# More score blocks turned by DMA, and z turned by overlapping twos, in a gated attention and token mixing kernel

## The chip, the core and the metric

The kernel runs on one core of one Trainium2 chip. The metric is the device time of one execution in microseconds; the median of several runs is compared. The core has the engines PE (TensorE: matmuls), DVE (VectorE), ACT (ScalarE), POOL (GpSimd) and SP (SyncE, which here only issues DMAs), and 16 DMA engines that all queues share. PEld in a profile is TensorE's loading of weights, which overlaps its matmuls.

## The reference

Eight batches (B), 3200 rows each (S), D = 256 columns; z and the two key projections have 64 columns.

```python
scores = (1 / S) * z @ z.T                  # S x S, symmetric
attn   = np.maximum(scores, 0.0) ** 2       # symmetric too
x      = u * (attn @ v)                     # S x D
wq, wk = x @ w_q, x @ w_k                   # S x 64
mixed  = ((1 / 8) * wq @ wk.T) @ x          # computed as wq @ (wk.T @ x)
out    = np.maximum(mixed, 0.0) @ w_out
```

All inputs and the output are float32; the kernel works in float16 with float32 sums. Since `attn` is symmetric, the block of rows i and columns j is the transpose of the block of rows j and columns i.

## The kernel before

**Tiling.** The 3200 rows of a batch are 25 tiles of 128 (row tiles). The columns of `attn` are cut into seven groups: six of 512 and a last one of 128 (`widths`, `starts`; `LASTG` is 6). For each batch `b` and group `gi`, all 25 row tiles are summed into the group's output: 4 x 25 = 100 steps of the second product for a full group, 25 for the last. One step is a pair of matmuls on the two halves of TensorE's rows, 64 rows each (`second_product`, line 332).

**Scores.** A score tile is 128 rows by the 512 columns of a group. Two tiles form a pair `p`; `scores` (line 247) gives one to the upper 64 rows of TensorE and one to the lower 64. For that z must stand transposed in both halves: `zT[b]`. The pair is evacuated by `first_stage` (ReLU, line 269 on ACT or 273 on DVE) and squared into float16 by `second_stage` (line 289 on ACT or 291 on POOL) into a buffer `at` of the pool `pat` (`NAT` = 14 pairs).

**Turned blocks.** Where `is_turned(b, gi, gj)` holds, the score tiles of group gi whose rows belong to group gj are also transposed by DMA on SP's queue (line 311), and serve as the tiles of group gj whose rows belong to gi, which are then not computed. Before the change it holds for groups one and two apart (`FAR` = 2) and for every group with the last. The turned blocks stand in buffers `tt1` (3), `tt2` (4) and `ttl` (8); a full block is 4 KiB in each partition.

**z of the next batches.** `load_z` brings z of batch b+1 by a converting DMA from POOL's queue, `double_z` copies it twice on DVE into `zd` (line 161), so that each tile stands there twice side by side, and `turn_z` transposes it in five DMAs of five tiles (line 167), which gives each tile in both halves at once.

**The rest of a group.** `gate` adds the two halves' sums (ACT line 348, DVE line 349) and multiplies by u (POOL line 370) into x. `turn_x` transposes x by DMA (line 384), `projections` (line 401) makes queries and keys, `turn_keys` (line 419) transposes the keys by DMA, POOL doubles them (line 431), `heads` (line 438) sums keys times x. When a batch is through, `mix` (line 466) and `proj` (line 493) make the output, ACT scales it (line 521), SP stores it (line 522). u is loaded by SP (line 175), v by POOL's queue (line 150).

**Order of the work.** The program is straight-line: a planner in Python runs through it while it is built, with a clock for each engine, SP's queue (`sp_at`) and the DMA engines (`dma_at`), and writes out each engine's instructions in the order that its estimates give. `use_pair` issues a pair of scores, `acc_step` a step of the second product. A transfer on SP is given to `move(ready, due, issue, takes, fn, landed, may)`; `flush` sends those that are ready, the earliest due first, and those with `may` only when that holds. `out_of[p]` counts transposes of pair p that have not landed; pair p may be produced only when the buffer of pair p - `NAT` is used up and turned. Scores run ahead of the second product: the pair is wanted when `p * total < (done_acc + lead) * NPAIR`, with `lead` = 140 steps.

Of the kernel before, what the change touches and what calls it, by code (L numbers as in the profile page):

```python
# [16 lines left out]
def kernel(  # L17
# [15 lines left out]
    P = 128  # L33
# [17 lines left out]

    NAT = 14
    NX = 6
    NEARBY = 8
# [7 lines left out]
    pk = ctx.enter_context(tc.tile_pool(name="pk", bufs=3))  # L62
    pxt = ctx.enter_context(tc.tile_pool(name="pxt", bufs=3))
    pu = ctx.enter_context(tc.tile_pool(name="pu", bufs=2))
# [21 lines left out]

    zT, vs, us, xs, xTs, qks, ks, hacc, hss, rts, zds = ({} for _ in range(11))

# [7 lines left out]
    z32 = {}  # L96
    zd0 = pz.tile([P, NT, 2, dqk], FP16, tag="zd", name="zd")
    vs[0] = pv.tile([P, NT, D], FP16, tag="v_sb", name="v_sb")
    zT[0] = pzt.tile([P, S], FP16, tag="zT2", name="zT2")

# [50 lines left out]

    zdense, ztimes = {}, []

    def load_z(b):
        zdense[b] = pz.tile([P, NT, dqk], FP16, tag="zn", name="zn")
        nc.gpsimd.dma_start(out=zdense[b][:], in_=rows(z, b))

    def double_z(b, half):
        if half == 0:
            zds[b] = pz.tile([P, NT, 2, dqk], FP16, tag="zd", name="zd")  # L160
        nc.vector.tensor_copy(out=zds[b][:, :, half, :], in_=zdense[b][:])

    def turn_z(b, i):
        ztimes.append((b, i))
        if i == 0:
            zT[b] = pzt.tile([P, S], FP16, tag="zT2", name="zT2")
# [11 lines left out]

    wq32 = consts.tile([P, NC, dh], FP32, tag="wq32", name="wq32")
    wk32 = consts.tile([P, NC, dh], FP32, tag="wk32", name="wk32")  # L180
    wqk = consts.tile([P, NC, 2, dh], FP16, tag="wqk", name="wqk")
# [57 lines left out]
    NPAIR = NTILE // 2  # L239
    made, turned = {}, {}  # L240

    def scores(p):
        assert len(ztimes) >= 5 * tiles[2 * p + 1][0] and p_chunk(p) in z_at, (p, clock, len(ztimes), z_at)
        sc = ps_tile("sc")
        for h, (b, gi, ti) in enumerate(tiles[2 * p : 2 * p + 2]):
            gs, gw = starts[gi], widths[gi]
            nc.tensor.matmul(  # L247
                out=sc[:, h, 0:gw],
                lhsT=zT[b][top(h), ts(ti, P)],
                rhs=zT[b][top(h), ds(gs, gw)],  # L250
                start=True,
                stop=True,
            )
        return sc
# [24 lines left out]
    def second_stage(p, g, ways):  # L279
        at = pat.tile([P, 2 * W], FP16, tag="at", name="at")  # L280
        at0 = 0
        parts = pieces(p)
        if len(ways) > len(parts):
            parts = [(slice(h, h + 1), parts[0][1]) for h in range(2)]
        for (hs, w), on_act in zip(parts, ways * 2):
            n = hs.stop - hs.start
            out = at[:, at0 : at0 + n * w].rearrange("p (n w) -> p n w", w=w)
            if on_act:
                nc.scalar.square(out=out, in_=g[:, hs, 0:w])  # L289
            else:  # L290
                nc.gpsimd.tensor_mul(out=out, in0=g[:, hs, 0:w], in1=g[:, hs, 0:w])  # L291
# [12 lines left out]
        def turn(b, gi, gj, n0, nn, c0, c1):  # L304
            if (b, gi, gj) not in turned:
                kind, nr, bufs = ("l", 1, 8) if gj == LASTG else (gj - gi, 4, gj - gi + 2)
                turned[b, gi, gj] = ptt.tile(
                    [P, nr, 4, P], FP16, tag=f"tt{kind}", name=f"tt{kind}", bufs=bufs
                )
            out = turned[b, gi, gj][:].rearrange("p n j t -> p (n j) t")  # L310
            nc.sync.dma_start_transpose(out=out[:, 4 * n0 : 4 * (n0 + nn), :], in_=at[:, c0:c1])

        return [(x, lambda x=x: turn(*x)) for x in blocks]
# [28 lines left out]
    def gate(b, gi, half):  # L342
# [9 lines left out]
        if b == last and gi >= LASTG - 2:  # L352
            if gi == LASTG - 2 and half == 0:
                spare = pz.tile([P, NT, 2, dqk], FP16, tag="zd", name="xd")
                spare = spare[:].rearrange("p n a k -> p (n a k)")
                spare = spare[:, 0 : 9 * D].rearrange("p (n d) -> p n d", d=D)
                for i in range(3):
                    xds[LASTG - 2 + i] = spare[:, 4 * i : min(4 * i + 4, 9), :]
# [21 lines left out]
    def turn_x(b, gi):  # L380
        assert len(xTs) < 3
        n = min(2, widths[gi] // P)
# [190 lines left out]
    sp_at, dma_at = [0.0], [0.0]  # L573
    LANDS = 4.0
    RING = 2.0
    SLACK = 1.0
# [41 lines left out]
    def cold():  # L618
        return 2.0 if clock[PE] < 8.4 else 1.0

    SPLIT = 0.2
    UNTIL = 24.0
# [27 lines left out]
    def squares():  # L650
        while pending and pending[0][0] <= clock[PE] + 0.3:
# [9 lines left out]
            for (b, gi, gj, _, nn, _, _), turn in second_stage(p, g, ways):  # L661
                n = nn * widths[gi] // P
                due = done + (4.0 if gj == gi + 1 else 9.0)
                out_of[p] = out_of.get(p, 0) + 1
                move(done + SLACK, due + SLACK, 1.28, 0.21 * n, turn, lambda t, x=(p, b, gi, gj, nn): block_landed(t, *x))
            for x in tiles[2 * p : 2 * p + 2]:
# [16 lines left out]
    def use_keys(b, gi):  # L683
# [15 lines left out]
        if not final:  # L699
            move(  # L700
                done + SLACK, done + 10.0, 1.28, 0.21 * n, lambda: turn_keys(b, gi),
                lambda t: at_time(t, lambda: double(b, gi)),
# [48 lines left out]
    def use_proj(b, gi):  # L751
# [12 lines left out]

        move(done + SLACK, done + 6.0, 0.55, 1.6, stores[0], landed)

# [3 lines left out]

    Z0 = 24
    V0 = 56
    V1 = 11

    def batch_begun(b, t):
        if b + 1 < B:
            t0 = max(t + 6, Z0)
            at_time(t0, lambda: (load_z(b + 1), push(3.0)))
            for half in range(2):
                at_time(  # L780
                    t0 + 12 + 3 * half,
                    lambda half=half: (double_z(b + 1, half), give(DVE, clock[PE], 0.98)),
                )
            step = 6 if b else 4
            for i in range(5):
                move(
                    t0 + 18 + step * i, t0 + 34 + step * i, 1.28, 1.05,
                    lambda i=i: turn_z(b + 1, i),
# [6 lines left out]
    def v_loaded(b, n0, nn):  # L795
        load_v(b, n0, nn)
        push(2.5)
        for n in range(n0, n0 + nn):
# [4 lines left out]
    def z_here(p):  # L803
        b = tiles[2 * p + 1][0]
        return not b or z_ready.get((b, 4), 1e9) <= clock[PE]

    def group_begun(b, gi, t):
        if gi == 0:
            batch_begun(b, t)
        if gi + 1 < NG:  # L810
            move(max(t + 2, clock[POOL] + SLACK), t + 7, 0.55, 1.6, lambda: load_u(b, gi + 1))
        elif b + 1 < B:
            move(max(t + 2, clock[POOL] + SLACK), t + 7, 0.55, 1.6, lambda: load_u(b + 1, 0))

    SPARE = 0.3
    BIAS = 0.2
    XDUE = 5.0
    XWAIT = 3.0
    LATE = 0.3
# [3 lines left out]
    def half_done(b, gi, half):  # L823
# [10 lines left out]
        elif half == halves(gi)[-1]:  # L834
            n = 8 if widths[gi] == W else 2
            move(
                t + SLACK, t + XDUE, 1.28, 0.21 * n, lambda: turn_x(b, gi),
                lambda t: x_landed(t, b, gi), lambda: len(xTs) < 3,
            )
# [54 lines left out]
    def acc_step():  # L894
# [59 lines left out]
    at_time(10.0, lambda: turn_first(3))  # L954
    move(10.0, 14.0, 0.55, 1.6, lambda: load_u(0, 0))
    load_weights()
# [3 lines left out]
    done_acc = 0  # L960
    lead = 140
    turn_about = False
    while groups or work or current["left"]:
# [134 lines left out]
```

## Time and profile before

| | before |
|---|---|
| median of 3 runs | 784.35 us (782.85 to 785.14) |
| profiled execution | 784.44 us |
| its span, first to last instruction | 782.7 us |
| granted TensorE clock | 0.999 |
| PE / PEld busy | 769.8 / 663.7 us |
| DVE / ACT / POOL busy | 503.3 / 546.4 / 645.1 us |
| transposes on SP: tt, ttl, xT_sb, kx, zT | 143, 48, 56, 53, 35 |
| DMA | 140.88 MB, 180 GB/s in the mean |

The profile is one execution. Busy time is the union of an engine's instructions. A group's row gives the line, the engine, the operation, output and inputs, the count, then busy us, the mean ns of one, and the engine's idle time just before these instructions with what ended it. The chain of work that ended last follows the span back from its end through what released each step. Transposes are issued on SP ("SPq"): the duration shown there is that of issuing; "to landing" is from issue until the data is there.

### The profile page before, as it was taken

The page shows a single profiled execution, that of the slowest core. Times are in us where ns is not written, and L with a number is a line of the kernel's source. Part 1 is how long each engine was busy: PE and PEld are TensorE (multiplying, and loading weights), DVE is VectorE, ACT ScalarE, POOL GpSimd, SP SyncE. Part 2 cuts the span into 40 slices and gives each one's busy share as a digit, 9 for nine tenths or more (in the row PEclk, how much of TensorE's full clock was granted, in tenths as well). Part 3 has the DMA queues.
Part 4 walks back from the last instruction along what each step waited for, and adds up shares of the span by engine and source line. Part 5 has one row for each costly group of instructions (what it writes and reads, how often), then busy time and mean ns, then how long its engine had stood idle before and what let it go on. Part 6 is the DMA issues. An engine that isn't in the chain of part 4 may idle for free.

```text
span 782.7 us, 28343 instructions
## 1 busy us (share of the span) xinstructions
PE 769.8 (98%) x12410; PEld 663.7 (85%) x12410; DVE 503.3 (64%) x515; ACT 546.4 (70%) x663; POOL 645.1 (82%) x530
## 2 busy tenths in 40 slices
PE   7999999999999999999999999999999999999996
PEld 5899999788899878888889887998889888898784
DVE  6766556655587556786476665777567556566635
ACT  6868777668676767766677767776678676777534
POOL 7898988788889877888789889778788879888961
PEclk9999999999999999999999999999999999999999
DMA  7999999999999999999799989999999998969635
GB/s 179 143 174 170 157 181 180 165 175 206 216 174 177 211 184 189 185 212 189 180 177 174 220 173 201 168 164 217 190 188 152 183 228 166 202 127 210 142 59 213
DMA packets 306300, 140.88 MB, mean 180 GB/s; under 512 B 285056, under 2 KB 287744, under 8 KB 306176
## 3 DMA queue, kind: packets, MB, share of 16 engines
q1 hardware_dynamic: 299408, 122.90, 82.1%
q0 software_dynamic: 6624, 15.98, 15.0%
q8 instruction: 97, 1.59, 0.9%
q10 hardware_dynamic: 144, 0.20, 0.1%
q14 instruction: 27, 0.22, 0.1%
HBM read 59.64 MB, written 26.21 MB: 110 GB/s over the span
## 4 chain that ended last, share of the span: by engine, by line
PE 92%; DVE 2%; DMA 1%; ACT 1%; POOL 1%; issue 1%; DVEq 0%; SPq 0%; ACTq 0%
PE acc L332 67%; PE sc L247 13%; PE fo L493 6%; PE qk L401 3%; PE qk L438 2%; PE mx L466 1%; DVE g L273 1%; DMA v_sb<-in_v_dram 1%; POOL at L291 1%; ACT g L269 1%; ACT at L289 0%; DMA z<-in_z_dram 0%; DVE fo L516 0%; PE hd L438 0%; DVE both L349 0%
## 5 line engine op out<-in xcount | busy, mean ns | idle before, releaser
L291 POOL TENSOR_TENSOR at<-g 128x1024 f16<-128x1024 f32 (+2 forms) x252 | 457.1, 1827 | 62.4 <-DVE g L273 50.3
L332 PE MATMUL acc<-v_sb,at 64*128 64x256 f16 x7344 | 498.4, 269 | 1.2 <-DMA v_sb<-in_v_dram 0.7
L273 DVE TENSOR_SCALAR g<-sc 128x1024 f32<-128x1024 f32 (+2 forms) x320 | 372.6, 1178 | 135.3 <-PE sc L247 126.7
L332 PEld LDWEIGHTS <-at 64*128 64x128 f16 x7344 | 400.9, 94 | 55.2 <-issue 8.1
L289 ACT ACTIVATE at<-g 128x1024 f16<-128x1024 f32 (+2 forms) x230 | 228.1, 1008 | 19.2 <-DVE g L273 17.0
L269 ACT ACTIVATE g<-sc 128x1024 f32<-128x1024 f32 (+2 forms) x159 | 156.5, 986 | 67.1 <-PE sc L247 58.5
L247 PE MATMUL sc<-zT 64*128 64x512 f16 x924 | 187.6, 377 | 1.9 <-DVE g L273 0.8
L370 POOL TENSOR_TENSOR x_sb<-both,u_sb 128x512 f16<-128x512 f32 (+1 forms) x112 | 134.7, 1209 | 43.9 <-DVE both L349 43.6
L332 PE MATMUL acc<-v_sb,tt 64*128 64x256 f16 x2272 | 159.2, 269 | 0.0
L332 PEld LDWEIGHTS <-tt 64*128 64x128 f16 x2272 | 123.5, 94 | 14.3
L349 DVE TENSOR_TENSOR both<-acc,both 128x512 f32<-128x512 f32 (+1 forms) x104 | 69.7, 670 | 86.4 <-ACT both L348 73.3
L348 ACT COPY both<-acc 128x512 f32<-128x512 f32 (+1 forms) x104 | 59.0, 568 | 70.7 <-PE acc L332 66.4
L247 PEld LDWEIGHTS <-zT 64*128 64x128 f16 x924 | 60.8, 94 | 12.9 <-issue 8.9
L521 ACT ACTIVATE fo<-fo 128x1024 f32<-128x1024 f32 (+1 forms) x48 | 44.6, 930 | 24.3 <-PE fo L493 23.8
L493 PE MATMUL fo<-wo,rt 128*128 128x256 f16 x400 | 53.2, 274 | 1.3 <-ACT rt L481 0.5
L483 ACT ACTIVATE rt<-mx 128x1024 f16<-128x1024 f32 (+1 forms) x49 | 45.6, 934 | 11.5 <-PE mx L466 11.2
L414 ACT CAST qk<-qk 128x512 f16<-128x512 f32 (+1 forms) x54 | 29.4, 544 | 30.0 <-PE qk L438 24.1
L493 PEld LDWEIGHTS <-rt 128*128 128x128 f16 x400 | 34.9, 98 | 15.8 <-issue 10.9
L453 DVE TENSOR_TENSOR ha<-qk,ha 128x512 f32<-128x512 f32 x37 | 25.6, 691 | 30.7 <-ACT qk L414 30.2
L401 PE MATMUL qk<-xT_sb,wqk 64*128 64x256 f16 (+1 forms) x404 | 32.4, 265 | 0.0
L431 POOL COPY kx<-kx 128x128 f16<-128x128 f16 (+1 forms) x99 | 26.2, 294 | 5.7 <-DMA kx<-qk 5.7
L438 PE MATMUL qk<-x_sb,kx 64*128 64x256 f16 x342 | 28.4, 269 | 0.0
(45 smaller groups left out, 233.7 us busy)
## 6 DMA issues: line engine op xcount, KB each, us to landing
u_sb<-in_u_dram SPq DMA_DIRECT2D x48, 512.0 KB, 4.9
out_dram<-fo SPq DMA_DIRECT2D x47, 512.0 KB, 5.2
v_sb<-in_v_dram POOLq DMA_DIRECT2D x35, 320.0 KB, 5.5
zn<-in_z_dram POOLq DMA_DIRECT2D x7, 400.0 KB, 6.8
tt<-at SPq DMA_TRANSPOSE x143, 4.3
u_sb<-in_u_dram SPq DMA_DIRECT2D x8, 128.0 KB, 3.1
out_dram<-fo SPq DMA_DIRECT2D x8, 128.0 KB, 3.4
xT_sb<-x_sb SPq DMA_TRANSPOSE x56, 5.8
```

Of the source, the lines that this page charges most:

```text
L247: nc.tensor.matmul(out=sc[:, h, 0:gw], lhsT=zT[b][top(h), ts(ti, P)], rhs=zT[b][top(h), ds(gs, gw)], start=True, stop=True,)
L269: nc.scalar.activation(out=g[:, hs, 0:w], in_=sc[:, hs, 0:w], func=RELU, scale=GSCALE)
L273: nc.vector.tensor_scalar(out=g[:, hs, 0:w], in0=sc[:, hs, 0:w], scalar1=0.0, scalar2=GSCALE, op0=AOP.max, op1=AOP.mult,)
L289: nc.scalar.square(out=out, in_=g[:, hs, 0:w])
L291: nc.gpsimd.tensor_mul(out=out, in0=g[:, hs, 0:w], in1=g[:, hs, 0:w])
L332: nc.tensor.matmul(out=accs[half, r][:, ds((j % 2) * D, D)], lhsT=weights(b, gi, ti, j)[top(r), :], rhs=vs[b][top(r), ti, :], start=(first ...
L348: nc.scalar.copy(out=both[:, 0 : n * D], in_=accs[half, 0][:, 0 : n * D])
L349: nc.vector.tensor_add(out=both[:, 0 : n * D], in0=accs[half, 1][:, 0 : n * D], in1=both[:, 0 : n * D])
L370: nc.gpsimd.tensor_mul(out=xs[b, gi][:, 0:n, :, r, :].rearrange("p n c d -> p (n c) d"), in0=both[:, 0 : n * D].rearrange("p (m d) -> p m ...
L401: nc.tensor.matmul(out=ps[:, r, 0 : n * P], lhsT=wqk[top(r), c, :, :].rearrange("p t h -> p (t h)"), rhs=xTs[b, gi][top(r), 0:n, c, :], st ...
L483: nc.scalar.activation(out=out, in_=ps[:, 0:nr, 0 : ND * n * P], func=RELU)
L493: nc.tensor.matmul(out=banks[r][:, ds(j * D, D)], lhsT=flat[:, ds((dc * n + j) * P, P)], rhs=wo[:, dc, :], start=(dc == 0 and j == 0), sto ...
```

## The change

- `EXTRA`: in batches 1 to 7 the blocks (0,3), (1,4), (2,5) and (0,4) are turned too; the score tiles that they stand for are not computed.
- **Homes.** Full turned blocks of every distance share `NHOME` = 7 buffers. A turn is sent only when its block has a home or one is free (`has_home`); the home comes back when the planner has issued the last step that reads the block (`give_home_back`).
- **z.** The copies on DVE are gone. z is loaded into one buffer `zn` with an empty tile before and after it (set to zero once, on POOL). Four transposes take twos of neighbouring tiles: those beginning at an even place, and those at an odd one. So each tile stands once in the upper and once in the lower half, the upper one 128 columns further on (`z_cols`).
- **Buffers.** `NAT` 14 to 16, `NX` 6 to 7, turned x 3 to 4 (`NXT`). The first batch's doubled z and the last x share the pool of v, the query and key weights that of the output tiles.
- **Planner.** The cost of a transposed block is 0.17 instead of 0.21 (`BLOCK`), of u and output rows 1.3 instead of 1.6 (`ROWS4`), of the v and z loads 1.8 and 2.2 instead of 2.5 and 3.0. Blocks three or four groups apart are due 12 us after their square. x waits 7 instead of 3 us before its keys. A pair is wanted by its place in its own group (`need`) instead of evenly over the run.

```diff
-    NAT = 14
-    NX = 6
+    NAT = 16
+    NX = 7
+    NXT = 4
...
     def load_z(b):
-        zdense[b] = pz.tile([P, NT, dqk], FP16, tag="zn", name="zn")
-        nc.gpsimd.dma_start(out=zdense[b][:], in_=rows(z, b))
-
-    def double_z(b, half):
-        if half == 0:
-            zds[b] = pz.tile([P, NT, 2, dqk], FP16, tag="zd", name="zd")
-        nc.vector.tensor_copy(out=zds[b][:, :, half, :], in_=zdense[b][:])
+        nc.gpsimd.dma_start(out=zn[:, 1 : NT + 1, :], in_=rows(z, b))
...
+    ZTURNS = [(0, 0, 7), (1, 0, 7), (0, 7, 13), (1, 7, 13)]
     def turn_z(b, i):
+        odd, m0, m1 = ZTURNS[i]
...
         nc.sync.dma_start_transpose(
-            out=zT[b][:].rearrange("p (n s) -> p n s", s=P)[:, 5 * i : 5 * i + 5, :],
-            in_=zds[b][:, 5 * i : 5 * i + 5, :, :].rearrange("p n a k -> p (n a k)"),
+            out=zT[b][:].rearrange("p (m o s) -> p o m s", o=2, s=P)[:, odd, m0:m1, :],
+            in_=zn[:, 2 * m0 + odd : 2 * m1 + odd, :].rearrange("p n k -> p (n k)"),
         )
+
+    def z_cols(b, h, at, n):
+        return zT[b][top(h), ds(at + (P if b and h == 0 else 0), n)]
...
     SKIP = [(0, 2)]
+    EXTRA = [(0, 3), (1, 4), (2, 5), (0, 4)]
     def is_turned(b, gi, gj):
         if b == 0 and (gi, gj) in SKIP:
             return False
+        if b and (gi, gj) in EXTRA:
+            return True
         return gi < gj and (gj <= gi + FAR or gj == LASTG)
...
+    NHOME = 7
+    homes, homes_free = {}, list(range(NHOME))
+
+    def has_home(b, gi, gj):
+        return gj == LASTG or (b, gi, gj) in turned or bool(homes_free)
+
+    def give_home_back(b, gj, t):
+        gi = group_of(t)
+        if (b, gi, gj) in homes and all(
+            (b, gj, starts[gi] // P + n) in used for n in range(widths[gi] // P)
+        ):
+            homes_free.append(homes.pop((b, gi, gj)))
...
-                lhsT=zT[b][top(h), ts(ti, P)],
-                rhs=zT[b][top(h), ds(gs, gw)],
+                lhsT=z_cols(b, h, ti * P, P),
+                rhs=z_cols(b, h, gs, gw),
...
-                kind, nr, bufs = ("l", 1, 8) if gj == LASTG else (gj - gi, 4, gj - gi + 2)
+                if gj == LASTG:
+                    tag, nr, bufs = "ttl", 1, 8
+                else:
+                    homes[b, gi, gj] = home = homes_free.pop(0)
+                    tag, nr, bufs = f"tt{home}", 4, 1
...
-                due = done + (4.0 if gj == gi + 1 else 9.0)
+                due = done + {1: 4.0, 2: 9.0}.get(gj - gi, FARDUE)
...
+                    lambda x=(b, gi, gj): has_home(*x),
...
-    XWAIT = 3.0
+    XWAIT = 7.0
...
         used.add(row)
+        if row:
+            give_home_back(*row)
...
+    for p in range(NPAIR):
+        b, gi, _ = tiles[2 * p]
+        i0, i1 = first_of[b, gi], ends[b, gi]
+        n = NT * (widths[gi] // P)
+        need.append(steps[b, gi] + STRETCH * n * (2 * p - i0) / (i1 - i0))
...
-        wanted = able and p * total < (done_acc + lead) * NPAIR
+        wanted = able and need[p] < done_acc + lead
```

`steps[b, gi]` is the number of second-product steps ahead of that group, `first_of` and `ends` are the places of a group's first and last tile in the list.

More of the change, by code (lines that the diff above doesn't have):

```diff
@@ L85 @@
     ctx.enter_context(tc.manual_schedule())
-    zT, vs, us, xs, xTs, qks, ks, hacc, hss, rts, zds = ({} for _ in range(11))
+    zT, vs, us, xs, xTs, qks, ks, hacc, hss, rts = ({} for _ in range(10))
     def rows(t, b):
@@ L96 @@
     z32 = {}
-    zd0 = pz.tile([P, NT, 2, dqk], FP16, tag="zd", name="zd")
+    zd0 = pv.tile([P, NT, 2, dqk], FP16, tag="v_sb", name="zd")
     vs[0] = pv.tile([P, NT, D], FP16, tag="v_sb", name="v_sb")
-    zT[0] = pzt.tile([P, S], FP16, tag="zT2", name="zT2")
+    zT[0] = pzt.tile([P, S + P], FP16, tag="zT2", name="zT2")
+    zn = pz.tile([P, NT + 2, dqk], FP16, tag="zn", name="zn")
     def load_first_z():
@@ L150, in load_v @@
         nc.gpsimd.dma_start(out=vs[b][:, n0 : n0 + nn, :], in_=rows(v, b)[:, n0 : n0 + nn, :])
[L152 removed]
+    ztimes = []
+    ZTURNS = [(0, 0, 7), (1, 0, 7), (0, 7, 13), (1, 7, 13)]
     def load_z(b):
[L155 to L161 removed]
+        nc.gpsimd.dma_start(out=zn[:, 1 : NT + 1, :], in_=rows(z, b))
     def turn_z(b, i):
+        odd, m0, m1 = ZTURNS[i]
         ztimes.append((b, i))
         if i == 0:
[L166 removed]
+            zT[b] = pzt.tile([P, S + P], FP16, tag="zT2", name="zT2")
         nc.sync.dma_start_transpose(
[L168 to L170 removed]
+            out=zT[b][:].rearrange("p (m o s) -> p o m s", o=2, s=P)[:, odd, m0:m1, :],
+            in_=zn[:, 2 * m0 + odd : 2 * m1 + odd, :].rearrange("p n k -> p (n k)"),
+        )
+    def z_cols(b, h, at, n):
+        return zT[b][top(h), ds(at + (P if b and h == 0 else 0), n)]
     def load_u(b, gi):
@@ L175, in load_u @@
         nc.sync.dma_start(out=us[b, gi][:, 0:nn, :], in_=rows(u, b)[:, n0 : n0 + nn, :])
-    wq32 = consts.tile([P, NC, dh], FP32, tag="wq32", name="wq32")
-    wk32 = consts.tile([P, NC, dh], FP32, tag="wk32", name="wk32")
+    w32s = pg.tile([P, 2, W], FP32, tag="fo", name="w32s", bufs=2)
+    w32s = w32s[:, 0, :].rearrange("p (i c h) -> p i c h", i=2, h=dh)
+    wq32, wk32 = w32s[:, 0, :, :], w32s[:, 1, :, :]
     wqk = consts.tile([P, NC, 2, dh], FP16, tag="wqk", name="wqk")
@@ L240 @@
     made, turned = {}, {}
+    NHOME = 7
[8 more added lines that the diff above has]
+            homes_free.append(homes.pop((b, gi, gj)))
     def scores(p):
-        assert len(ztimes) >= 5 * tiles[2 * p + 1][0] and p_chunk(p) in z_at, (p, clock, len(ztimes), z_at)
+        assert len(ztimes) >= 4 * tiles[2 * p + 1][0] and p_chunk(p) in z_at, (p, clock, len(ztimes), z_at)
         sc = ps_tile("sc")
@@ L305, in turn @@
             if (b, gi, gj) not in turned:
-                kind, nr, bufs = ("l", 1, 8) if gj == LASTG else (gj - gi, 4, gj - gi + 2)
-                turned[b, gi, gj] = ptt.tile(
-                    [P, nr, 4, P], FP16, tag=f"tt{kind}", name=f"tt{kind}", bufs=bufs
-                )
+                if gj == LASTG:
[3 more added lines that the diff above has]
+                    tag, nr, bufs = f"tt{home}", 4, 1
+                turned[b, gi, gj] = ptt.tile([P, nr, 4, P], FP16, tag=tag, name=tag, bufs=bufs)
             out = turned[b, gi, gj][:].rearrange("p n j t -> p (n j) t")
@@ L353, in gate @@
             if gi == LASTG - 2 and half == 0:
-                spare = pz.tile([P, NT, 2, dqk], FP16, tag="zd", name="xd")
-                spare = spare[:].rearrange("p n a k -> p (n a k)")
-                spare = spare[:, 0 : 9 * D].rearrange("p (n d) -> p n d", d=D)
+                spare = pv.tile([P, NT, D], FP16, tag="v_sb", name="xd")
                 for i in range(3):
@@ L380, in turn_x @@
     def turn_x(b, gi):
-        assert len(xTs) < 3
+        assert len(xTs) < NXT
         n = min(2, widths[gi] // P)
@@ L574 @@
     LANDS = 4.0
+    BLOCK = 0.17
+    ROWS4 = 1.3
     RING = 2.0
@@ L619, in cold @@
         return 2.0 if clock[PE] < 8.4 else 1.0
+    FARDUE = 12.0
     SPLIT = 0.2
@@ L662, in squares @@
                 n = nn * widths[gi] // P
-                due = done + (4.0 if gj == gi + 1 else 9.0)
+                due = done + {1: 4.0, 2: 9.0}.get(gj - gi, FARDUE)
                 out_of[p] = out_of.get(p, 0) + 1
-                move(done + SLACK, due + SLACK, 1.28, 0.21 * n, turn, lambda t, x=(p, b, gi, gj, nn): block_landed(t, *x))
+                move(
+                    done + SLACK, due + SLACK, 1.28, BLOCK * n, turn,
+                    lambda t, x=(p, b, gi, gj, nn): block_landed(t, *x),
+                    lambda x=(b, gi, gj): has_home(*x),
+                )
             for x in tiles[2 * p : 2 * p + 2]:
@@ L763, in landed @@
             stored[i] = t
-        move(done + SLACK, done + 6.0, 0.55, 1.6, stores[0], landed)
+        move(done + SLACK, done + 6.0, 0.55, ROWS4, stores[0], landed)
     def push(takes):
@@ L771 @@
     Z0 = 24
+    ZWAIT, ZDUE, ZSTEP, ZSTEP0 = 14.0, 32.0, 7.0, 5.0
     V0 = 56
@@ L777, in batch_begun @@
             t0 = max(t + 6, Z0)
[L778 to L785, printed above, removed]
+            if b == 0:
+                nc.gpsimd.memset(zn[:, 0 : NT + 2 : NT + 1, :], 0.0)
+            at_time(t0, lambda: (load_z(b + 1), push(2.2)))
+            step = ZSTEP if b else ZSTEP0
+            for i, (_, m0, m1) in enumerate(ZTURNS):
                 move(
-                    t0 + 18 + step * i, t0 + 34 + step * i, 1.28, 1.05,
+                    t0 + ZWAIT + step * i, t0 + ZDUE + step * i, 1.28, BLOCK * (m1 - m0),
                     lambda i=i: turn_z(b + 1, i),
@@ L796, in v_loaded @@
         load_v(b, n0, nn)
-        push(2.5)
+        push(1.8)
         for n in range(n0, n0 + nn):
@@ L804, in z_here @@
         b = tiles[2 * p + 1][0]
-        return not b or z_ready.get((b, 4), 1e9) <= clock[PE]
+        return not b or z_ready.get((b, 3), 1e9) <= clock[PE]
     def group_begun(b, gi, t):
@@ L810, in group_begun @@
         if gi + 1 < NG:
-            move(max(t + 2, clock[POOL] + SLACK), t + 7, 0.55, 1.6, lambda: load_u(b, gi + 1))
+            move(max(t + 2, clock[POOL] + SLACK), t + 7, 0.55, ROWS4, lambda: load_u(b, gi + 1))
         elif b + 1 < B:
-            move(max(t + 2, clock[POOL] + SLACK), t + 7, 0.55, 1.6, lambda: load_u(b + 1, 0))
+            move(max(t + 2, clock[POOL] + SLACK), t + 7, 0.55, ROWS4, lambda: load_u(b + 1, 0))
     SPARE = 0.3
@@ L836, in half_done @@
             move(
-                t + SLACK, t + XDUE, 1.28, 0.21 * n, lambda: turn_x(b, gi),
-                lambda t: x_landed(t, b, gi), lambda: len(xTs) < 3,
+                t + SLACK, t + XDUE, 1.28, BLOCK * n, lambda: turn_x(b, gi),
+                lambda t: x_landed(t, b, gi), lambda: len(xTs) < NXT,
             )
@@ L954 @@
     at_time(10.0, lambda: turn_first(3))
-    move(10.0, 14.0, 0.55, 1.6, lambda: load_u(0, 0))
+    move(10.0, 14.0, 0.55, ROWS4, lambda: load_u(0, 0))
     load_weights()
@@ L961 @@
     lead = 140
+    STRETCH = 1.0
+    need, at, seen = [], 0, 0
+    steps = {}
+    for b in range(B):
+        for gi in range(NG):
+            steps[b, gi] = at
+            at += NT * (widths[gi] // P)
+    first_of = {}
+    for i, (b, gi, t) in enumerate(tiles):
+        first_of.setdefault((b, gi), i)
+    for p in range(NPAIR):
[3 more added lines that the diff above has]
+        need.append(steps[b, gi] + STRETCH * n * (2 * p - i0) / (i1 - i0))
     turn_about = False
```

4 lines of the change are left out of this document (2 added, 2 removed).

## The prediction

> **What bounds the kernel now.** I read the busy times first, then the chain of work that ended last, then the groups by line, the waits, the windows by stage, and last the queue of SP, because the change adds work there.
>
> ```profile
> PE 769.8 (98%) x12410; PEld 663.7 (85%) x12410; DVE 503.3 (64%) x515; ACT 546.4 (70%) x663; POOL 645.1 (82%) x530
> PE acc L332 67%; PE sc L247 13%; PE fo L493 6%; PE qk L401 3%; PE qk L438 2%; PE mx L466 1%; DVE g L273 1%; DMA v_sb<-in_v_dram 1%; POOL at L291 1%; ACT g L269 1%; ACT at L289 0%; DMA z<-in_z_dram 0%; DVE fo L516 0%; PE hd L438 0%; DVE both L349 0%
> ```
>
> 92% of that chain lies on TensorE: 67% in the second product (line 332), 13% in the scores (line 247). The other engines have room on average. The groups say whether TensorE waits for anybody:
>
> ```profile
> L332 PE MATMUL acc<-v_sb,at 64*128 64x256 f16 x7344 | 498.4, 269 | 1.2 <-DMA v_sb<-in_v_dram 0.7
> L332 PE MATMUL acc<-v_sb,tt 64*128 64x256 f16 x2272 | 159.2, 269 | 0.0
> L247 PE MATMUL sc<-zT 64*128 64x512 f16 x924 | 187.6, 377 | 1.9 <-DVE g L273 0.8
> L291 POOL TENSOR_TENSOR at<-g 128x1024 f16<-128x1024 f32 (+2 forms) x252 | 457.1, 1827 | 62.4 <-DVE g L273 50.3
> ```
>
> The idle column of the first three rows is 1.2, 0.0 and 1.9 us in the whole run: neither an evacuation nor a turned block (the `tt` row) makes TensorE wait. Most of the idle time lies at the two ends; one batch in the middle shows it, by the windows (columns: PE, weight loads, DVE, ACT, POOL, clock, DMA share, GB/s):
>
> ```profile
> 274.00:371.00 97.00, 97.00 (x1568) 82.15 (x1565) 67.12 (x67) 67.63 (x82) 81.19 (x66) 1.00 1.05 192
> 745.00:783.00 38.00, 31.09 (x430) 24.37 (x425) 17.71 (x23) 13.28 (x25) 12.46 (x14) 0.98 0.45 140
> ```
>
> TensorE is busy for all 97 us of the batch, at the full clock. A busy TensorE need not be at its peak, since matmuls overlap. The timeline of TensorE alone decides that (columns: start, us, instruction):
>
> ```profile
> 271.35 0.39 PE L247 MATMUL sc<-zT 64*128 64x512 f16 x2
> 271.57 1.36 PE L332 MATMUL acc<-v_sb,at 64*128 64x256 f16 x22
> 272.77 0.22 PE L466 MATMUL mx<-qk,hs 64*128 64x128 f16 x1
> ```
>
> A pair of score matmuls, whose halves run side by side, occupies 271.57 - 271.35 = 0.22 us. The 22 second-product matmuls after it take 1.20 us until the next starts, 0.109 us a pair. So 5000 pairs of the second product take 545 us and 462 pairs of scores 102 us. The order of instructions on each engine is written out by the planner before the run, so a score pair taken out closes the ranks behind it unless an operand comes late.
>
> **What it removes.** Group gi needs a score tile for each of 25 row tiles, less those it takes from an earlier group turned. By `is_turned` the counts by group are 25, 21, 17, 17, 17, 17, 1 (115 a batch), and with the four new blocks (0,3), (1,4), (2,5), (0,4) they are 25, 21, 17, 13, 9, 13, 1 (99). Sixteen tiles less in 7 batches are 112 tiles, 56 pairs; 924 matmuls become 812. The longer answer of the chain gives line 247 12.7% of 782.7 us, 99.4 us, which over 462 pairs is 0.215 us each; the timeline says 0.22. **56 x 0.215 = 12.0 us** (12.3 by the timeline). The second product is unchanged in number.
>
> The same 56 pairs leave the other engines: one first stage each (1221 ns on DVE or 1025 ns on ACT for 128x1024) and one square (1895 ns on POOL or 1055 ns on ACT). Also gone are 14 copies that double z on DVE, 975 ns each, 13.7 us. I count all of that at nothing: it lies beside TensorE, which waited 0.8 us on DVE there. It gives cover.
>
> A rule speaks against the price. The Trainium skill, Perfetto Trace Analysis, "Identifying the Most-Contended Engine", says that matmul busy time is no good measure of TensorE's headroom and that the busy share of weight loads is. By the page of the profile that share is 85%, and line 247's loads are busy for 60.8 us over 462 pairs, 0.13 us a pair, so by it the sum would be 56 x 0.13 = 7.4 us. The trace doesn't agree with it here, and I keep 0.215: the timeline shows that the missing loads are score pairs streaming 512 columns behind short loads, not idle time.
>
> **What it adds, all of it on SP and the DMA rings.** Each of the 28 new blocks is turned by two transposes of 128x1024:
>
> ```profile
> L311 SPq DMA_TRANSPOSE tt<-at x143: 1231/1267/5132, 18.6 to 724.4; - x143
> DMA to landing us min/median/max: 2.7/4.3/10.6
> SPq L311 <- POOL at L291: 42.4, 37, 5.1
> ```
>
> Columns of the first: issue time in ns, least, median and most. 56 more issues at 1.27 us are 71 us of SP; the z transposes go from 5 to 4 a batch (median 1287 ns), 7 x 1.29 = 9 us back. By the trace SP's issues fill 628 of 783 us now (mean 1.72 us for line 311: long ones are held up by full rings). At that mean the new total is 628 + 96 - 11 = 713 of 771 us, 92% instead of 80%. The packets' time, 98% of sixteen engines, isn't a capacity: stages run at 1.15 already (80 to 177 us). The blocks turned rise from some 2120 to 2570, a fifth.
>
> What hides it: a new block is made in group gi and read three or four groups later; a group lasts 97 / 6.25 = 15.5 us, so 30 us or more lie between, against 10.6 us for the slowest landing. Queued behind a waiting transpose on SP are the u loads, the x and key transposes and the stores. Their readers are POOL (line 370), TensorE (line 401) and POOL (line 431), which waited 0, 0.2 and 5.7 us for DMAs here. I take 0 us. The bounds: no gain, because nothing waits for less; and a loss up to the whole 12 us if each x transpose comes 1.7 us late and TensorE waits once a batch (7 x 1.7).
>
> **Homes.** Blocks got 3 buffers at distance one and 4 at distance two; now 7 homes serve all distances, and a turn is held by the planner until one is free. Counting lifetimes: by the time group 1's scores are made, (0,1) to (0,4) and (1,2) to (1,4) fill all seven. The blocks of group 2 must wait until groups 1 and 2 were summed, and (3,4), (3,5), (4,5) for the end of group 3. Until then they sit in the square buffers, now 16 pairs instead of 14. At group 3's end these hold some 15 pairs (4.5 of group 3, 4.5 of group 4, 6.5 of group 5). It fits with little to spare. Group 4 begins on its 9 own tiles and 12 that were turned long ago, 21 x 4 x 0.109 = 9.2 us of the second product and some 4 us of other work, before it needs (3,4): two issues of 1.27 us and a landing of 4.3 us are 6.8 us. I take 0; the price of being late is a rival below.
>
> **The rest, each about nothing.** z goes to its transposes undoubled, as overlapping twos of tiles: the same 128-column blocks, 26 instead of 25, and score operands shifted by 128 columns. One small memset on POOL: nearest row, the 128x128 copy of line 431 at 298 ns, once. x waits 7 instead of 3 us before its keys, a seventh x and a fourth turned x: no instruction. z, weights and the last x sit in other pools, whose earlier readers ended long before. Scores are paced within each group instead of evenly: this reorders TensorE's queue; TensorE's idle time by windows of 20 us is 2.1 us from 20 to 760 us, the most that order can win; what it can lose is in the rivals.
>
> **Sum.** The profiled execution took 784.44 us (span 782.7 and 1.7 around it), 0.1 above the median of 784.35. 784.4 - 12.0 = **772.4 us**.
>
> **Rivals.**
> 1. *Part of it comes back* as waits for SP's later transfers. For: SP at 92%, single issues of 5.1 us. Against: TensorE waited 0.0 us for `tt`. Half of the gain lost gives 778; 774 to 782. By the skill's weight-load measure it would be 777, in the same band.
> 2. *No net change*, 782 to 786.7: the bound moves to SP and the rings. For: the DMA share is above 1 in the middle batches. Against: its gaps; SP stood waiting for sources (42.4 us for POOL alone).
> 3. *Slower, by the homes.* If (3,4) and (4,5) land after the tiles ahead of them are used up, or the square buffers fill so that scores stop, TensorE stands at groups 4 and 5 of 7 batches, 14 places. Break-even is 12.0 / 14 = 0.9 us each. A landing of 10.6 us instead of 4.3 eats the 6 us of margin, and some 2 us at each place give 772.4 + 28 = 800. For: seven homes for ten blocks wanted. Against: most landings are near the median.
>
> That the scores aren't removed is no rival: the tile list leaves them out.
>
> **Numbers.** A measurement tells about 0.3% (2.35 us) from no change: faster is below 782.0, slower above 786.7. The forecast (769 to 774) 0.48, below 769 0.03, rival 1 0.22, rival 2 0.06, rival 3 0.21. Faster 0.73, same 0.06, slower 0.21. The range 769 to 789 holds the forecast, rivals 1 and 2 and the near end of 3 (0.05): 0.81.
>
> **What would show it.** Right: 812 matmuls on line 247, 406 pairs; the middle batches some 1.7 us shorter with TensorE still busy throughout; `tt` transposes near 199; idle before the `tt` matmuls still about 0; DVE some 55 us less busy. Rival 1: idle time before lines 332, 401 and 438 released by a DMA, SP issues longer than 1.72 us in the mean. Rival 3: gaps in TensorE late in each batch, ended by `tt` or by a square. The prediction is wrong if TensorE's idle time outside the ends rises by more than 2 us.

## The result and the profile after

The changed kernel takes **847.67 us** in the median of 5 runs (838.66 to 850.13), against 784.35 for the kernel before in the same session: 1.079 times as long (95% interval 1.074 to 1.084). The forecast was 772.4 us and faster. The profiled execution is the fastest of the five, 838.66 us with a span of 836.9 us. In all that follows, a run more than 1.5% above the fastest run of its kernel counts as slow and is left out of medians and ratios.

The busy times on the page of the changed kernel:

```profile
PE 776.4 (93%) x12298; PEld 660.7 (79%) x12298; DVE 444.0 (53%) x464; ACT 498.4 (60%) x613; POOL 599.8 (72%) x506
```

Its chain of work that ended last, by engine and by line:

```profile
PE 63%; DMA 14%; POOL 11%; issue 5%; ACT 3%; DVE 2%; SPq 1%; DVEq 0%; POOLq 0%; ACTq 0%
PE acc L352 45%; POOL at L309 8%; PE sc L265 7%; DMA kx<-qk 6%; PE fo L511 4%; DMA out_dram<-fo 3%; POOL x_sb L388 3%; PE qk L419 2%; PE qk L456 2%; DMA xT_sb<-x_sb 2%; DVE g L291 1%; PE mx L484 1%; ACT g L287 1%; DMA tt<-at 1%; DMA v_sb<-in_v_dram 1%
```

TensorE held 92% of that chain and now holds 63%; transfers and POOL came in. DVE, ACT and POOL are all less busy than before. What has more work is the DMA path: 155.77 MB instead of 140.88. The groups (busy us, mean ns, then idle time before and what ended it; the first row is of the kernel before):

```profile
L431 POOL COPY kx<-kx 128x128 f16<-128x128 f16 (+1 forms) x99 | 26.2, 294 | 5.7 <-DMA kx<-qk 5.7
L352 PE MATMUL acc<-v_sb,at 64*128 64x256 f16 x6448 | 441.2, 273 | 11.2 <-POOL at L309 10.3
L352 PE MATMUL acc<-v_sb,tt 64*128 64x256 f16 x3168 | 209.2, 272 | 0.0
L265 PE MATMUL sc<-zT 64*128 64x512 f16 x812 | 163.2, 379 | 2.3 <-DVE g L291 1.2
L449 POOL COPY kx<-kx 128x128 f16<-128x128 f16 (+1 forms) x99 | 25.9, 290 | 104.6 <-DMA kx<-qk 104.5
L419 PE MATMUL qk<-xT_sb,wqk 64*128 64x256 f16 (+1 forms) x404 | 33.7, 275 | 10.7 <-DMA xT_sb<-x_sb 6.4
L456 PE MATMUL qk<-x_sb,kx 64*128 64x256 f16 x348 | 30.1, 281 | 6.8 <-POOL kx L449 6.8
```

The scores went down to 812 matmuls as forecast, and TensorE doesn't wait for the turned blocks themselves (0.0 on the `tt` row). The late ones are older transfers on the same path: POOL stood 104.5 us for turned keys, against 5.7 us before. One such place, on SP first, then on POOL and on TensorE (start, us, instruction, idle time before it):

```profile
208.31 1.27 SPq L402 DMA_TRANSPOSE xT_sb<-x_sb  x1
209.62 0.57 SPq L176 DMA_DIRECT2D u_sb<-in_u_dram  x1
210.29 0.38 SPq L540 DMA_DIRECT2D out_dram<-fo  x1
210.76 1.75 SPq L437 DMA_TRANSPOSE kx<-qk  x1
212.56 2.36 SPq L331 DMA_TRANSPOSE ttl<-at  x1
```

```profile
211.85 0.59 POOL L158 DMA_DIRECT2D zn<-in_z_dram  x1
212.46 1.91 POOL L309 TENSOR_TENSOR at<-g 128x1024 f16<-128x1024 f32 x1
219.17 0.53 POOL L449 COPY kx<-kx 128x128 f16<-128x128 f16 x2 [4.80 <-DMA kx<-qk]
219.66 3.74 POOL L309 TENSOR_TENSOR at<-g 128x1024 f16<-128x1024 f32 x2
```

```profile
223.46 3.17 PE L352 MATMUL acc<-v_sb,at 64*128 64x256 f16 x28 [4.47 <-POOL at L309]
```

The key transpose is issued at 210.76 and by the trace lands only at 219.12, 8.4 us later (median before 4.1). POOL's doubling of keys stands in front of two squares in POOL's order, so POOL stands still for 4.80 us with squares that could have been made; TensorE needs one of those squares and stops for 4.47 us. TensorE's next instruction asked for a square, not for the key: the late key stops it by way of another engine's order.

Keys are not the only way, nor the costliest. The stores of the output are late too. ACT fills one of two tiles `fo` once an earlier store has landed, and TensorE's `mix` waits for ACT (who waited for whom: us in total, times, longest):

```profile
ACT fo L539 <- DMA out_dram<-fo: 26.4, 7, 6.0
PE mx L484 <- ACT fo L539: 13.8, 4, 5.4
```

Neither wait is in the trace of the kernel before. TensorE's longest stop, 5.41 us from 288.56 us, is one of these: the store issued at 285.20 landed by the trace at 293.45. By the waits in the trace TensorE stood 19.6 us for ACT's `fo` (13.8 for line 484, 4.3 for line 419, 1.5 for line 511), 10.3 us for POOL's squares, 6.8 us for doubled keys and 6.4 us for turned x.

The windows show what a stop costs besides itself (columns as before; the figure after POOL's is the granted clock; the last line is of the kernel before):

```profile
200.00:220.00 20.00, 18.99 (x308) 14.94 (x302) 12.42 (x13) 16.33 (x20) 15.18 (x16) 1.00 1.01 176
220.00:240.00 20.00, 16.54 (x237) 14.42 (x239) 9.26 (x9) 9.39 (x12) 15.67 (x12) 0.83 1.07 220
30.00:792.00 762.00, 713.38 (x11434) 610.40 (x11430) 404.25 (x412) 459.73 (x551) 563.47 (x466) 0.97 1.07 188
30.00:738.00 708.00, 706.63 (x11542) 614.23 (x11538) 462.18 (x465) 507.72 (x600) 603.30 (x486) 1.00 1.02 183
```

From 222.19 us, near the end of the stop, the clock is granted at 0.5 for 6.83 us (0.83 over the window). By the trace there are nine such stretches in the middle of the run, of 3.41 or 6.83 us, 41 us together at half clock. Each goes with a stop of TensorE of 2.06 to 5.41 us (one with two stops close together, 1.55 and 2.69 us); the five single stops of 1.52 to 1.85 us have none. The Trainium skill, TensorE: Matmul & The Clock Gate, "Part 1: The HAM clock gate", says that an idle window of about 3.4 us halves the clock. This trace agrees on the length, with its stretches of 3.41 us, but stops of 2.06, 2.85 and 3.32 us were already enough.

**The account.** From 30 us to 792 us TensorE idles 762 - 713.4 = 48.6 us; before it was 1.4 us from 30 to 738 us. In 6.5 of the 41 us at half clock it stood idle anyway; half of the other 34.4 us, 17.2 us, is an estimate of what the clock costs. 47.2 + 17.2 = 64.4 us of loss, less the 13.5 us that 56 score pairs are worth (measured below), are 50.9 us. The spans differ by 836.9 - 782.7 = 54.2 us, so some 3 us stay unexplained.

### The profile page after: what moved, and what is told of

Read it like the earlier page. It is cut to its first block, busy times and chain, and to the rows that moved or that the text cites. A ratio compares the mean times of both kernels' runs of the same rounds, so it can differ in the third digit from the quotient of the medians.

```text
span 836.9 us, 28030 instructions
## 1 busy us (share of the span) xinstructions
PE 776.4 (93%) x12298; PEld 660.7 (79%) x12298; DVE 444.0 (53%) x464; ACT 498.4 (60%) x613; POOL 599.8 (72%) x506
## 2 busy tenths in 40 slices
DMA packets 366107, 155.77 MB, mean 186 GB/s; under 512 B 344865, under 2 KB 347553, under 8 KB 365985
## 4 chain that ended last, share of the span: by engine, by line
PE 63%; DMA 14%; POOL 11%; issue 5%; ACT 3%; DVE 2%; SPq 1%; DVEq 0%; POOLq 0%; ACTq 0%
PE acc L352 45%; POOL at L309 8%; PE sc L265 7%; DMA kx<-qk 6%; PE fo L511 4%; DMA out_dram<-fo 3%; POOL x_sb L388 3%; PE qk L419 2%; PE qk L456 2%; DMA xT_sb<-x_sb 2%; DVE g L291 1%; PE mx L484 1%; ACT g L287 1%; DMA tt<-at 1%; DMA v_sb<-in_v_dram 1%
## 5 line engine op out<-in xcount | busy, mean ns | idle before, releaser
L352 PE MATMUL acc<-v_sb,at 64*128 64x256 f16 x6448 | 441.2, 273 | 11.2 <-POOL at L309 10.3
L309 POOL TENSOR_TENSOR at<-g 128x1024 f16<-128x1024 f32 (+2 forms) x227 | 410.0, 1819 | 51.0 <-DVE g L291 41.0
L291 DVE TENSOR_SCALAR g<-sc 128x1024 f32<-128x1024 f32 (+2 forms) x283 | 325.4, 1167 | 199.1 <-PE sc L265 176.3
L352 PEld LDWEIGHTS <-at 64*128 64x128 f16 x6448 | 350.5, 95 | 63.9 <-POOL at L309 12.2
L352 PE MATMUL acc<-v_sb,tt 64*128 64x256 f16 x3168 | 209.2, 272 | 0.0
L307 ACT ACTIVATE at<-g 128x1024 f16<-128x1024 f32 (+2 forms) x199 | 195.3, 1000 | 16.4 <-DVE g L291 14.6
L352 PEld LDWEIGHTS <-tt 64*128 64x128 f16 x3168 | 167.1, 95 | 21.5 <-issue 1.2
L265 PE MATMUL sc<-zT 64*128 64x512 f16 x812 | 163.2, 379 | 2.3 <-DVE g L291 1.2
L287 ACT ACTIVATE g<-sc 128x1024 f32<-128x1024 f32 (+2 forms) x140 | 138.3, 989 | 41.7 <-PE sc L265 36.2
L449 POOL COPY kx<-kx 128x128 f16<-128x128 f16 (+1 forms) x99 | 25.9, 290 | 104.6 <-DMA kx<-qk 104.5
L265 PEld LDWEIGHTS <-zT 64*128 64x128 f16 x812 | 52.0, 95 | 12.4 <-issue 8.2
```

The source lines that it names most:

```text
L265: nc.tensor.matmul(out=sc[:, h, 0:gw], lhsT=z_cols(b, h, ti * P, P), rhs=z_cols(b, h, gs, gw), start=True, stop=True,)
L287: nc.scalar.activation(out=g[:, hs, 0:w], in_=sc[:, hs, 0:w], func=RELU, scale=GSCALE)
L291: nc.vector.tensor_scalar(out=g[:, hs, 0:w], in0=sc[:, hs, 0:w], scalar1=0.0, scalar2=GSCALE, op0=AOP.max, op1=AOP.mult,)
L352: nc.tensor.matmul(out=accs[half, r][:, ds((j % 2) * D, D)], lhsT=weights(b, gi, ti, j)[top(r), :], rhs=vs[b][top(r), ti, :], start=(first ...
```

## The experiments

Times are medians. The kernels with long waits scatter, so the ratio to the kernel before is given with its 95% interval. Three theories were set against each other. *Queue*: the added transposes overload the path of transfers, whatever becomes of their blocks. *Costs*: the planner's lower estimates alone make the order too tight. *Homes and z*: waits for homes, or the new turning of z, hold up SP.

**No extra blocks.**

```diff
-    EXTRA = [(0, 3), (1, 4), (2, 5), (0, 4)]
+    EXTRA = []
```

> The changed kernel with the list of extra blocks empty: homes, z by twos, 16 buffers, the planner's new costs and the pacing stay, and all 924 score matmuls are back. Queue theory (the 56 added transposes fill SP's queue, so that the transfers behind them come late): SP has its 328 transposes and its gaps again, the key transposes no longer make POOL wait 100 us, and the time is 780 to 792. Rival, cost theory (the planner's lower costs of a transfer alone make the order too tight): it stays above 810. Rival, z or homes theory (the turning of z by twos, or waits for homes, hold the queue): above 810 too.

Measured: 794.56 us, 1.011 (1.005 to 1.017). 53 of the 63 us are gone with the blocks. It lies 2.6 us above the band expected, and POOL still waited 55.5 us for keys: something smaller remains.

**Old costs in the planner, extra blocks kept.**

```diff
-    BLOCK = 0.17
+    BLOCK = 0.21
-    ROWS4 = 1.3
+    ROWS4 = 1.6
...
-            at_time(t0, lambda: (load_z(b + 1), push(2.2)))
+            at_time(t0, lambda: (load_z(b + 1), push(3.0)))
...
-        push(1.8)
+        push(2.5)
```

> The changed kernel with the planner's old costs of transfers (block 0.21, rows 1.6, loads 3.0 and 2.5), extra blocks kept. Cost theory: an order made with honest costs removes the waits of TensorE for late transfers, and the time falls under 800, perhaps to 775. Queue theory: the transposes themselves need the time that the old costs say (8 x 0.21 = 1.68 us, measured mean 1.69), so the order only becomes looser and the time stays at 835 to 870.

Measured: 836.83 us, 1.063 (1.056 to 1.070). Eleven microseconds better and no more. The waits only move, by the groups of this kernel (its profiled execution took 842.85 us):

```profile
L352 PE MATMUL acc<-v_sb,tt 64*128 64x256 f16 x3168 | 223.4, 272 | 11.2 <-DMA tt<-at 11.1
L449 POOL COPY kx<-kx 128x128 f16<-128x128 f16 (+1 forms) x99 | 25.7, 288 | 19.2 <-DMA kx<-qk 19.0
```

An order that expects longer transfers has the keys in time and the turned blocks late. The cost theory falls for the extra blocks.

**Idle turns: the transposes without the use.** All score matmuls are computed; the same squares are turned into buffers that nobody reads. To make room for them, `NAT`, `NX` and `NXT` are back at 14, 6 and 3.

```diff
+            if b and (gi, gj) in IDLE:
+                spare = ptt.tile([P, 2, 4, P], FP16, tag="idle", name="idle", bufs=4)
+                out = spare[:].rearrange("p n j t -> p (n j) t")
+                nc.sync.dma_start_transpose(out=out[:, 0 : 4 * nn, :], in_=at[:, c0:c1])
+                return
```

> No extra blocks are used, all 924 score matmuls are computed, but the same squares are also turned into four spare buffers that nobody reads (buffer counts as in the kernel before, 14, 6 and 3, to make room). Queue theory: 56 or a few more transposes cost as much here as in the changed kernel although nothing reads them; SP over 95% busy through the middle, 835 to 865, that is some 60 above the kernel without extra blocks. Homes theory (waits for homes or late turned blocks are what costs): no reader, no home, so 780 to 800.

Measured: 852.39 us, 1.085 (1.077 to 1.092). That is 57.8 us above the kernel without extra blocks, **1.03 us for each of 56 idle transposes**, though the blocks turned need no home and have no reader. So the whole loss comes without homes for them, and the homes theory falls. The two kernels also differ in the buffer counts, and part of the 57.8 us could come from there; the next experiment compares kernels with equal buffers.

**Half as much in each idle turn.** This is an edit of the kernel with idle turns; the buffers stay.

```diff
-                nc.sync.dma_start_transpose(out=out[:, 0 : 4 * nn, :], in_=at[:, c0:c1])
+                nc.sync.dma_start_transpose(out=out[:, 0 : 2 * nn, :], in_=at[:, c0 : (c0 + c1) // 2])
```

> The kernel with the idle turns, each idle turn moving half as many blocks (4 of 128x128 instead of 8); as many issues on SP. If a transpose costs by its blocks (DMA time), the 60 us over the kernel without extra blocks are halved: 820 to 830. If it costs by the issue, it stays at 846 to 860.

Measured: 821.72 us, 1.043 (1.039 to 1.048): 27.2 us above the kernel without extra blocks instead of 57.8. The count of issues is the same, so the cost goes by the blocks moved, 0.12 to 0.13 us each (27.2 / 224 and 57.8 / 448), not by the issue. Between the two idle kernels, which have the same buffers, it is 30.7 / 224 = 0.14 us.

**Stores issued by ACT.**

```diff
-        proj_out(b, gi, ps, [(False, nc.sync, widths[gi] // P)], stores)
+        proj_out(b, gi, ps, [(False, nc.scalar, widths[gi] // P)], stores)
...
-        move(done + SLACK, done + 6.0, 0.55, ROWS4, stores[0], landed)
+        stores[0]()
+        give(ACT, done, 0.1)
+        landed(done + 6.0)
```

> The changed kernel with the 55 stores of the output inside the batches issued by ACT right behind the instruction that makes them, so SP's queue loses 55 issues of 0.5 us and their waits; the bytes moved are the same. If SP's issuing is the limit, about 30 us of issue and its share of held-up time go, and the time falls to 790 to 820. If the DMA rings or engines are the limit, it stays within 10 us of 847.

Measured: four runs from 834.27 to 855.34 us, around those of the changed kernel (838.66 to 850.13): no change that can be told, and far from the 790 to 820 that a limit in SP's issuing would have given. By the trace 48 stores moved to ACT.

**No loads of v, no loads of u, neither.** These leave out transfers on another queue, on SP's queue, and on both, so that the output is made from the wrong v or u.

```diff
-        if n0 == 0:
-            vs[b] = pv.tile([P, NT, D], FP16, tag="v_sb", name="v_sb")
-        nc.gpsimd.dma_start(out=vs[b][:, n0 : n0 + nn, :], in_=rows(v, b)[:, n0 : n0 + nn, :])
+        vs[b] = vs[0]
```

```diff
+        if b or gi > 1:
+            us[b, gi] = kept_u[gi % 2]
+            return
```

> The changed kernel without the 35 loads of v for batches 1 to 7 (batch 0's v is used for all, so those loads are left out and the output of batches 1 to 7 is made from the wrong v); the order of everything else is the same. If the transposes share a limited DMA path with POOL's loads (a transpose stream that stands still while a v load is under way), most of the loss goes: 775 to 800. If the limit is the stream of transposes on SP's queue alone, the time stays over 830.

> The changed kernel with only the first two of the 56 loads of u (their tiles serve all groups, so x is made from the wrong u; 54 loads on SP left out); the planned order is the same. If the transposes share the 16 DMA engines with everything that moves, leaving out these 26 MB helps about as much as leaving out the 35 loads of v did: 785 to 805. If it is the loads on POOL's queue in particular that hold up transposes, the time stays at 825 to 848.

> The changed kernel without the loads of v for batches 1 to 7 and without 54 of the 56 loads of u (both left out as before, wrong v and u used). If the price of the score pairs in the prediction was right and only the DMA path ate it, the forecast of the prediction comes true here: 769 to 776. If the changed order of TensorE has a cost of its own (homes, the square buffers, the pacing), it stays above 780.

Measured: without v 789.18 us, 1.003 (0.999 to 1.007); without u 794.45 us, 1.011 (1.007 to 1.014); without both **769.01 us** (768.62 to 769.31), 0.979 (0.973 to 0.984). Leaving out 35 loads on POOL's queue or 54 on SP's gives back 53 to 59 us, though every transpose stays: the stream of transposes alone is not the limit, and neither is POOL's queue in particular. Without both the order of the changed kernel runs without a stop, by the groups of the kernel without both:

```profile
L355 PE MATMUL acc<-v_sb,at 64*128 64x256 f16 x6448 | 434.3, 269 | 0.9 <-DMA v_sb<-in_v_dram 0.6
L355 PE MATMUL acc<-v_sb,tt 64*128 64x256 f16 x3168 | 206.7, 269 | 0.0
L452 POOL COPY kx<-kx 128x128 f16<-128x128 f16 (+1 forms) x99 | 25.6, 287 | 3.3 <-DMA kx<-qk 3.3
```

and by the window of its middle:

```profile
30.00:722.00 692.00, 691.51 (x11410) 604.63 (x11406) 403.15 (x411) 457.29 (x548) 541.76 (x430) 1.00 0.87 155
```

TensorE idles 0.5 us in 692, at the full clock. With that much of the path free, homes, square buffers and pacing cost nothing that shows. The Trainium skill, DMA: Bandwidth & Descriptors, "Issuing engines are not separate DMA queues", says that DMAs of all engines run on the same 16 DMA engines and interleave; the runs without v and with ACT's stores agree.

**The kernel before, without the same loads.**

> The kernel before the change, with the same loads left out: v of batches 1 to 7 and 54 of the 56 loads of u (wrong v and u used). If the kernel before is bound by TensorE, its time hardly moves, 779 to 785, and the distance to the changed kernel without those loads (769.0) is the price of 56 score pairs, 12 us. If it too was held by the DMA path, it falls to 770 to 775.

Measured: 782.50 us (782.23 to 782.79), 0.995 (0.993 to 0.998). The kernel before was bound by TensorE: free of those 54 + 35 loads it gains about 3 us. The distance 782.5 - 769.0 = **13.5 us** is what 56 score pairs are worth: TensorE's busy time falls as much, from 768.8 to 755.4 us, and it is 769.2 us in the next kernel, which has the rest of the change but the planner's costs.

**No extra blocks and old costs.**

> The changed kernel without extra blocks and with the planner's old costs of transfers: what is left of the change is z by twos, homes, buffers and the pacing. If the 9 us by which the kernel without extra blocks lies above the one before come from the planner's costs, this lies at 780 to 787; if they come from the homes, z by twos or the pacing, it stays at 790 to 797.

Measured: 786.23 us, 0.999 (0.996 to 1.003). So the 8 us that the kernel without extra blocks lies above this one come from the planner's lower estimates (the intervals just part), and z by twos, homes, buffers and pacing together change nothing that can be told. This is as fast as the kernel before, not faster; no version tried that computes everything beat it.

**One extra block, used and idle.**

> The changed kernel with one extra block a batch, (2,5), instead of four: 14 transposes and 14 score pairs less than the half. If every added transpose costs the same 1.1 us against 0.215 us for each pair saved, the time is 794.6 + 14 x 0.85 = 806.5 (802 to 811). If the queue absorbs a few and only breaks down beyond, 785 to 796.

> The kernel with idle turns, but of the block (2,5) alone: 14 idle transposes a run, read by nobody, and all score matmuls computed. The kernel with (2,5) as a used extra block took 819. If the transposes alone make that cost, this takes 3 us more than it, 815 to 825. If it comes from the use of the block (a home late, a turned block late), this takes 794.6 and up to 15 us for 14 x 1.07: 796 to 810.

Measured: (2,5) used 818.97 us, 1.039 (1.033 to 1.046); (2,5) turned and not used 805.5 us from two runs (800.90 and 810.03), 1.025 (1.014 to 1.036). Above the kernel without extra blocks that is 24.4 and 10.9 us for 14 transposes. The first was expected at 802 to 811 and missed: the first 14 blocks are not free, and they cost more each than 56 do. The idle one is 0.8 us for each transpose, with a wide interval, and lies in the band that was expected if the use of the block makes the cost. The used block takes 13.5 us longer than the idle one though it saves 14 score pairs, and the two intervals hardly overlap, so it may well have a price of its own. Its trace shows no wait of TensorE on the `tt` row (0.0); its longest stops, 7.7 and 4.9 us, are of `mix` for ACT's `fo`. The two kernels also differ in buffers. What the difference is stays open.

## Why the prediction was wrong

- **What bounds the kernel: right**, and shown by the kernel before without loads, which moved by 0.5%.
- **The price of the score pairs: right in size.** 12.0 us forecast, 13.5 us measured (0.24 us a pair instead of 0.215). By the share of weight loads, one of the two measures of headroom that the Trainium skill names (Perfetto Trace Analysis, "Identifying the Most-Contended Engine"), it would have been 7.4 us; the runs don't agree with that.
- **What it adds: the step that failed.** "I take 0 us" for 56 transposes on SP and the DMA rings. With all score matmuls still computed, 56 transposes that nobody reads cost 57.8 us. The working saw SP rising to 92%, and dismissed the packets' 98% of sixteen engines as no capacity because stages ran at 1.15. It asked whether the *new* blocks would be late, found 30 us of slack, and was right about that (0.0 us on `tt`). It gave the *old* transfers behind them a mere bound of 12 us, by guessing how late an x transpose would be; the runs show 0.12 to 0.13 us for each added block. The sign of being wrong that it set itself came: TensorE's idle time outside the ends rose from 1.4 to 48.6 us.
- **Readers of those transfers.** It counted as harmless that POOL waited 5.7 us for keys. POOL's order has squares behind that wait; it became 104.5 us and reached TensorE through them. It named the stores as queued behind, but no reader for them: ACT's tiles `fo` wait for stores to land, and through them TensorE lost 19.6 us, the most of any way. POOL's wait by itself does not measure the loss: it was 55.5 us without extra blocks and 55.3 us with half idle turns, 27 us of time apart.
- **The clock.** Not in the prediction at all: the longer stops bring 3.41 or 6.83 us at half clock each, an estimated 17.2 us in sum, about a quarter of the loss.
- **Homes** (rival 3, which lay nearest with 800): not the mechanism. The idle turns lose as much without homes for the blocks; only the 13.5 us of the one used block stay open.
- **Rival 2** named the right mechanism, the bound moving to SP and the rings, and stopped its price at no change, as if the loss couldn't exceed the gain. With the lower costs told to the planner, the order was made for transfers of 1.36 us (8 x 0.17) where an issue took 1.69 us in the mean; about that mean was in the trace of before (1.72 for line 311). Higher costs took off only 11 us.
- **The rest at nothing: right**, for z, homes, buffers and pacing without the extra blocks (786.23 us). The planner's costs were left out of that sum; they cost about 8 us.

## What to carry to other kernels

A mean can hide that a path is full. Before the change SP was issuing for 80% of the span and hardly anybody waited for what it issued, and still the added transfers cost about their full time. Price every added transfer at its full time on the path (here 0.12 to 0.13 us for a 128x128 block in float16) until a run shows that it's free. Slack of the new transfer is not the question; ask who is queued behind it, and what stands behind *their* readers in each engine's order, and which buffers wait for a store to land. And two experiments settle such a case quickly: issue the new transfers with nobody reading them, and leave out other transfers to see whether the forecast then comes true.

## What the runs showed of the hardware

- Transposes slow down while other transfers are under way. In the changed kernel the trace shows 280 packets of 256 bytes in a quarter of a microsecond while transposes run alone (280.5 to 281.5 us), and 47 in the 3 us from 276.5 to 279.5 us, with a v load issued at 272.09 and landed at 280.44 and three transposes outstanding. That is an extreme place. Counted over the run from 40 to 777 us, half microseconds with a transpose outstanding (issued 2 us ago or more) hold 327 such packets in the mean with no other load or store under way, 150 with a load of POOL's queue, 170 with a u load or a store, and 100 with both. That v's and u's loads cost time is shown by leaving them out (58 and 53 us); what inside the DMA engines makes the transposes wait was not tried.
- A turn of eight blocks moves 128 x 1024 values of 2 bytes, 1024 packets of 256 bytes. At the rate of transposes alone that is an estimated 0.9 us, not far from the 1.03 us that each idle turn cost.
- The path's mean throughput hardly rose when more was asked of it: 140.88 MB at 180 GB/s before, 155.77 MB at 186 GB/s after; free of stops, without v and u, it ran at 155 GB/s (134 in the kernel before without them). That 180 GB/s of this mix was near what the path can do is argued from this and not shown: single slices of the page of the changed kernel stand at up to 248 GB/s.
